# Agent attention and a soft mixture of experts: joining partition maxima by masked products instead of copies, with later combine steps

## The chip, the cores and the metric

The kernel runs on one core of a Trainium2 chip. The metric is the time of one execution on the device in microseconds (us), given as the median of several runs. A profile shows one further execution in detail. Its engines are TensorE (PE; its weight loads are listed as PEld), VectorE (DVE), ScalarE (ACT), GpSimd (POOL) and SyncE (SP), which here only issues transfers. Everything is in 32-bit floating point.

## The reference

B = 4 batches, N = 11456 tokens each, C = 128 channels, 49 agents, 8 experts of 4 slots each (32 slots) and a hidden width of 1024.

```python
def sm(a, b):
    s = scale * (a @ b.transpose(0, 2, 1))
    s = s - s.max(-1, keepdims=True)
    e = np.exp(s)
    return e / (e.sum(-1, keepdims=True) + 1e-09)
agent_v = sm(agents, k) @ v              # agents look at all tokens
x = sm(q, agents) @ agent_v              # tokens look at the agents
...
logits = x @ phi                         # (B*N, 32)
d = softmax of logits over all tokens    # dispatch
slot_input = d.T @ x
for e in range(E):
    h = np.maximum(slot_input[e] @ w1[e], 0.0)
    slot_out[e] = h @ w2[e]
c = softmax of logits over the 32 slots  # combine
return c @ slot_out
```

So there are three softmaxes: over all keys of a batch (49 rows), over the 49 agents for every token, and two over the logits, one down all 45824 tokens and one across the 32 slots. The first and the dispatch one need a maximum that runs over partitions as well as along them.

## The kernel before

**Layout.** The tokens of a batch are cut into four streams. A cell is 32 tokens of each stream, so 128 tokens, and a batch has 90 cells. A group is 16 cells (10 in a batch's last), so a batch has six groups of keys and six of queries, 24 of each in all. With 32 columns of weights, four products write the four quadrants of 32 partitions of one PSUM tile, one for each stream.

**Key side, one group** (function `k_ops`; names as in the order list): `kx` and `kv` load, `ks` makes scores of 64 padded agents in two halves of 32 (line 219), `km` takes the negated maximum of each half along the row (L249). The four quadrants hold the same agents for different tokens, so their maxima must be joined and the result spread to all quadrants again. `kt` moves three quadrants' values to the first with three ScalarE copies (L255), `kr` reduces them together with the running maximum (L261, VectorE), `kn` spreads the result with three more ScalarE copies (L267). Then `ke` takes exponentials (L272), `ka` the rescaling factor, `kT` transposes on VectorE (L283), `kE` multiplies with the values (L290), and `kA` accumulates. After a batch's last group `kg` and `kh` form the agents' values and their product with phi.

**Query side, one group** (`q_ops`): `qx` load, `qs` scores, `qt` transposes, `qm` maxima, then either `qE` (exponentials on ScalarE cell by cell with a sum, L430) or `qu`, `qe`, `qd` (GpSimd, ScalarE, VectorE); `qw`, `qr`, `qN` normalise, `qp` and `qc` transpose through TensorE, `ql` makes the logits (L466), `qM` takes their maximum along the row (L479), `qv` transposes them into a buffer `lt` (L471). The combine softmax follows: `cr` maxima over the slots (L484, VectorE), `cu` subtraction into the result array `x_all` (L487, GpSimd), `ce` exponential in place (L492, ScalarE).

**Rounds** (`r_ops`). One or two query groups form a round, 13 in all. `r2` brings the quadrants' logit maxima together (three ScalarE copies, L536), `r3` reduces (L539), `r4` spreads (three copies, L544), `r5` transposes, `ru`, `re`, `rg` subtract, exponentiate and multiply into the dispatch sums, which `rc` copies out.

**Tail.** The rounds are rescaled to a common maximum, the slot inputs go through the experts (`mh`, `mr`, `mt`, `mc`, `mo`), and `sob` holds the slots' outputs. The output loop then runs over 24 chunks of 16 cells (8 in the first and the last two): `o_sum`, `o_eps`, `o_rec`, `o_mul` normalise the combine weights in `x_all`, `o_tr` transposes them, four products make an output tile of four PSUM banks (L933), VectorE copies one bank (L937), ScalarE three (L938), and a store follows (L942). The first 6 chunks' `o_sum` to `o_mul` (token names `os`, `oe`, `or`, `om`) and 4 transposes (`ot`) stand ahead of the loop.

**The order.** Every engine executes its instructions in the order in which they are issued. That order is written out by hand in a list of tokens, `ORDER` (lines 48 to 101). It holds all steps up to the output loop. Each step names what it depends on, and which buffer it takes and gives back (`BUFS`). The loads are in this list too, and go through SyncE's queue.

Of the kernel before, what the change touches and what calls it, by code (L numbers as in the profile page):

```python
# [7 lines left out]
F32 = mybir.dt.float32  # L8
# [46 lines left out]
ke.1 kx kT.0 qu qe km.1 qE.0 kT.1 km.0 ka@3 qE.3 qe kE kt ka kr kn kA qd ks.1 kE kA qw ke.0 km.1
kt kv ks.0 ka kx ke.1 qd kT.0 qN qE.1 qw@5 kr qw qc.0 qr ks.1 km.0 kT.1 km.1 qp.1@2 kn kE kv cx
kA kt qc.1 qp.0 ke.0 qN qp.1 kA qp.0 ks.0 qc.1@2 qc.0 qr kT.0 ke.1 kT.1 kE qc.1 ka kr kn ke.0 kA
qx km.0 ks.1 km.1 kg.1 kh.1 kt kT.0 kg.2 qp.1 ke.1 kr qx kh.2 kh.5 kg.3 kh.4 kT.1 kh.3 qs.0 qt.0
qr kn qs.1 ql qt.1 ql qm qs.0 qc.0 qv qN kx ke.0 kx qs.1 qE.2 ka ks.0 qu qM qt.0 qE.3 kT.0 ks.1
ke.1 qc.1 qt.1 kv ql qN qp.0 kx qv qc.0 km.0 qM km.1 r2 qp.1 kT.1 qM qc.1 cr ks.0 kt r3 ql qe kr  # L60
ks.1 kn qM qm kv ke.0 ke.1 km.0 cu qp.0 km.1 qv kE r4 kA kx ks.0 qE.0 r5 qp.1 qd kT.0 qc.0 kt qw
kr ql r2 qE.1 ka kn ks.1 r3 ru.0 kT.1 qw kE qr qr km.0 ka kv ke.0 ke.1 qv kv qM qc.1 ks.0 qE.2
qN@7 ks.1 km.1 qN kt kT.0 ru.1 ql r4 kE km.0 kr qE.3 kn qx km.1 re.0 kT.1 kA qM cr@3 kt qv@5 kA
kE r2 kr ke.0 kx qv qw qr kx cr ke.1 r3 qp.0@7 kT.0 r5 qp.1 qN ka kn qc.0@7 qp.0 rg.0 qc.0 ka
qs.0 qs.1 kT.1 ce qc.1 qt.0 qt.1 qp.0 r4 ke.0 ks.0 kT.0 ke.1 ru.0 qm qu re.1 cu@3 ks.1 km.0 ks.0
kv qc.0 km.1 km.0 kT.1 rg.1 re.0 ks.1 kv qx@11 kt kA cr qp.1 ce@3 qe qx kr km.1 cu ru.1 kn qc.1
kx cr ke.0 qd kE qw kE cr qx ke.1 kt kx qr kT.0 qs.0@11 kA kA cu@4 qN qs.1@11 rc kr qp.1@6 kg.1
qt.0@11 qt.1@11 r5 kg.2 cu qm@11 re.1 qc.1@6 qp.0 kn rg.0 ru.0 kh.1 kT.1 qs.0 kv ce qx ke.0 kh.2
kT.0 qt.0 qs.1 kh.5 kh.4 qt.1 kg.3 qu kh.3 qp.1 kv rg.1 qm ql ks.0 qM ke.1 km.0 re.0 ks.1 qs.0
qv qe qc.0 ru.1 km.1 qE.0 ql re.1 qc.1 qs.1 qd ql qt.0 kT.1 kt ql rc qM qt.1 qx kr qE.1 qM qE.2  # L70
qE.3 qw kn qv@8 qm qr qw r2 kx qM qv qr rg.0 ke.0 ks.0 rg.1 rc r3 ka@14 qE.0 kE ke.1 r2 r4 cu kA
ka qE.1 qN kT.0 km.0 cr r5 ks.1 qs.0 qN qs.1 qp.0 r3 ce@4 ru.0 cr r4 kT.1 km.1 qp.0 re.0 qt.0 kx
# [941 lines left out]
```

## Time and profile before

| what | us |
|---|---|
| median of 3 runs (lowest, highest) | 307.31 (306.68, 308.25) |
| the profiled execution's own time | 306.44 |
| its span in the profile | 304.6 |
| TensorE busy, its weight loads | 246.4, 126.4 |
| VectorE busy | 227.1 |
| ScalarE busy | 244.3 |
| GpSimd busy | 126.9 |

The span runs from the first to the last instruction in the trace; the execution's own time has 1.8 us more around it. Busy time is the union of an engine's instructions. A matmul's row is about 0.2 to 0.9 us long, but many overlap, so a group of matmuls takes far less than their number times that mean. In a row of a window, "x" gives the number of instructions, and a bracket at its end gives the engine's idle time before it and what ended it. In a row of groups, the two numbers before the second bar are busy time in us and the mean of one instruction in ns. In a row of waits, "X <- Y: total, times, longest" says for how long X stood idle until Y was done. A total of shares "by line" is of the chain of work that ended last, followed back through what released each step.

### The profile page before, as it was taken

The page shows a single profiled execution, that of the slowest core. Times are in us where ns is not written, and L with a number is a line of the kernel's source. Part 1 is how long each engine was busy: PE and PEld are TensorE (multiplying, and loading weights), DVE is VectorE, ACT ScalarE, POOL GpSimd, SP SyncE. Part 2 cuts the span into 40 slices and gives each one's busy share as a digit, 9 for nine tenths or more (in the row PEclk, how much of TensorE's full clock was granted, in tenths as well). Part 3 has the DMA queues.
Part 4 walks back from the last instruction along what each step waited for, and adds up shares of the span by engine and source line. Part 5 has one row for each costly group of instructions (what it writes and reads, how often), then busy time and mean ns, then how long its engine had stood idle before and what let it go on. Part 6 is the DMA issues. An engine that isn't in the chain of part 4 may idle for free.

```text
span 304.6 us, 8492 instructions
## 1 busy us (share of the span) xinstructions
PE 246.4 (81%) x3236; PEld 126.4 (42%) x3236; DVE 227.1 (75%) x490; ACT 244.3 (80%) x898; POOL 126.9 (42%) x136
## 2 busy tenths in 40 slices
PE   4668888999779998889998998979889965586830
PEld 1113245735463645434554364565665611121200
DVE  0567988499687999768998897788857599678620
ACT  2397899798997999989999999999967587566550
POOL 0010352231445833336742827568859134344200
PEclk9999999999999999979999999999979999556575
DMA  7999999999999997998999988729900079999996
GB/s 237 422 423 417 415 367 384 413 422 340 410 421 385 419 417 267 411 366 303 357 352 341 421 344 310 274 99 388 425 13 2 2 319 420 413 424 417 421 421 267
DMA packets 16023, 104.09 MB, mean 342 GB/s; under 512 B 1904, under 2 KB 2160, under 8 KB 4720
## 3 DMA queue, kind: packets, MB, share of 16 engines
q1 hardware_dynamic: 15840, 103.49, 84.9%
q8 instruction: 25, 0.41, 0.5%
q14 instruction: 14, 0.11, 0.1%
q10 hardware_dynamic: 144, 0.07, 0.1%
HBM read 79.96 MB, written 23.59 MB: 340 GB/s over the span
## 4 chain that ended last, share of the span: by engine, by line
ACT 37%; DMA 21%; PE 17%; DVE 15%; issue 4%; POOL 2%; SPq 2%; DVEq 0%; ACTq 0%
DMA out<-ot 10%; ACT pt L430 9%; DMA qt<-qT 7%; ACT es L272 5%; DMA w2s<-w 4%; PE sq L219 3%; ACT pT L460 3%; PE ev L290 3%; ACT mxs L267 3%; ACT mxs L255 2%; PE sk L219 2%; DVE ot L937 2%; ACT x_all L430 2%; DVE et L283 2%; PE tp L453 2%
## 5 line engine op out<-in xcount | busy, mean ns | idle before, releaser
L219 PE MATMUL sk<-kt,ag 128*32 128x512 f32 (+1 forms) x384 | 49.7, 588 | 12.4 <-DMA kt<-kT 6.1
L219 PE MATMUL sq<-qt,ag 128*32 128x512 f32 (+1 forms) x384 | 46.1, 572 | 7.7 <-DMA qt<-qT 3.9
L933 PE MATMUL po<-ct,sob 32*128 32x512 f32 (+1 forms) x192 | 35.8, 827 | 16.6 <-ACT ot L938 16.4
L938 ACT COPY ot<-po 128x1536 f32<-128x1536 f32 (+1 forms) x24 | 32.6, 1358 | 20.6 <-DVE ot L937 19.2
L430 ACT ACTIVATE pt<-pt,mx 128x49 f32<-128x49 f32 x144 | 46.4, 329 | 0.2
L290 PE MATMUL ev<-vt,et 128*64 128x129 f32 x720 | 44.3, 276 | 1.5 <-PE ev L290 0.9
L290 PEld LDWEIGHTS ev<-vt,et 128*64 128x64 f32 x720 | 39.3, 136 | 9.9 <-issue 3.9
L553 POOL TENSOR_TENSOR dt<-lt,mb 128x512 f32<-128x512 f32 (+1 forms) x24 | 29.2, 1226 | 33.0 <-DVE mb L548 14.1
L445 POOL TENSOR_TENSOR pt<-pt,rt 128x784 f32<-128x784 f32 (+1 forms) x19 | 26.6, 1400 | 28.4 <-DVE rt L441 22.5
L249 DVE TENSOR_REDUCE mxs<-sk 128x1 f32<-128x512 f32 (+1 forms) x48 | 30.4, 642 | 10.0 <-PE sk L219 9.4
L789 POOL TENSOR_TENSOR x_all<-x_all,cd 128x512 f32<-128x512 f32 (+1 forms) x24 | 23.8, 994 | 30.7 <-DVE cd L784 30.7
L283 DVE STREAM_TRANSPOSE et<-es 128x512 f32<-128x512 f32 (+1 forms) x48 | 31.3, 655 | 6.3 <-ACT es L272 6.0
L272 ACT ACTIVATE es<-sk,mxs 128x512 f32<-128x512 f32 (+1 forms) x48 | 30.7, 656 | 0.4
L460 ACT COPY pT<-tp 100x512 f32<-100x512 f32 (+1 forms) x48 | 25.7, 556 | 2.8 <-PE tp L453 2.0
L937 DVE COPY ot<-po 128x512 f32<-128x512 f32 (+1 forms) x24 | 15.6, 648 | 16.5 <-DMA out<-ot 14.3
L430 ACT ACTIVATION_READ_ACCUMULATOR pt<-pt,mx 128x1 f32 x144 | 27.8, 193 | 0.0
L933 PEld LDWEIGHTS po<-ct,sob 32*128 32x128 f32 x192 | 9.6, 234 | 42.5 <-ACT ot L938 42.0
L402 DVE STREAM_TRANSPOSE pt<-sq 128x512 f32<-128x512 f32 (+1 forms) x38 | 25.0, 657 | 2.3 <-PE sq L219 1.6
L487 POOL TENSOR_TENSOR x_all<-lt,rm 128x512 f32<-128x512 f32 (+1 forms) x24 | 23.7, 998 | 6.8 <-DVE m_all L539 4.6
L219 PEld LDWEIGHTS sk<-kt,ag 128*32 128x32 f32 x384 | 10.7, 110 | 31.7 <-ACT es L272 9.7
L453 PE MATMUL tp<-cs,pt 128*100 128x128 f32 x140 | 21.3, 286 | 2.7 <-DVE acc L296 2.3
L466 PE MATMUL lq<-pT,bd_m 100*32 100x256 f32 (+1 forms) x384 | 22.8, 367 | 0.5 <-ACT bd_m L334 0.3
(114 smaller groups left out, 425.2 us busy)
## 6 DMA issues: line engine op xcount, KB each, us to landing
out<-ot SPq DMA_DIRECT2D x21, 1024.0 KB, 7.4
vt<-vL SPq DMA_DIRECT2D x20, 1032.0 KB, 10.0
qt<-qT SPq DMA_DIRECT2D x20, 1024.0 KB, 9.4
kt<-kT SPq DMA_DIRECT2D x19, 1024.0 KB, 8.9
w2s<-w SPq DMA_DIRECT2D x4, 1024.0 KB, 7.6
w1s<-w SPq DMA_DIRECT2D x4, 1024.0 KB, 12.0
vt<-vL SPq DMA_DIRECT2D x4, 645.0 KB, 7.1
qt<-qT SPq DMA_DIRECT2D x4, 640.0 KB, 10.3
```

What stands on the lines that cost most here:

```text
L219: t_.matmul(sp[32 * q4:32 * q4 + 32, :nt], ag[:, b, 32 * h:32 * h + 32], xv[:, q4, :], start=True, stop=True)
L249: v_.tensor_reduce(out=mxs[i % 6][:, 2 * h, 0:1], in_=k["s"][h][:, :nt], axis=AX.X, op=ALU.max, negate=True)
L272: s_.activation(out=k["e"][:, h, :nt], in_=k["s"][h][:, :nt], func=AF.Exp, bias=k["nm"][:, 2 * h:2 * h + 1])
L283: v_.transpose(out=k["et"][:, :n, 32 * h:32 * h + 32], in_=k["e"][:, h, :nt].rearrange("p (t a) -> p t a", a=32))
L290: t_.matmul(k["ev"][o:o + 64, :], k["et"][:, c, :], k["v"][:, c, :], start=c < 2, stop=c >= n - 2)
L430: s_.activation(out=x, in_=x, func=AF.Exp, bias=q["mx"][:, c:c + 1], accum_out=q["rt"][:, c:c + 1])
L445: nc.gpsimd.tensor_tensor(out=x, in0=x, op=ALU.mult, in1=q["rt"][:, :n].unsqueeze(2).to_broadcast([P, n, A]))
L453: t_.transpose(q["tp", h][:, (c - h0) // 2, :], q["pt"][:, c:c + 2, :].rearrange("p c a -> p (c a)"), ident)
L460: s_.copy(out=q["pT"][:, h0 // 2:h1 // 2, :], in_=q["tp", h][:, :(h1 - h0) // 2, :])
L553: nc.gpsimd.tensor_tensor(out=q["dt"][:, :n], in0=q["lt"][:, :n, :], op=ALU.subtract, in1=r["mb"].unsqueeze(1).to_broadcast([P, n, S]))
L933: t_.matmul(po[:, r, :32 * n], z["sob"][32 * r:32 * r + 32, :], z["ct", j][32 * r:32 * r + 32, :32 * n], start=True, stop=True)
L938: s_.copy(out=ov[:, 1:4], in_=po[:, 1:4, :32 * n])
```

## The change

1. The key maxima. `km` writes into a small tile of two columns. A new step `kz` (VectorE) multiplies it with a mask, so that a 128 x 16 operand holds each quadrant's values in its own columns and zeros elsewhere. A new step `kb` (TensorE) multiplies that by a 128 x 32 matrix of stacked identities: four products bring all quadrants' values, and the running maximum, to all four quadrants of a PSUM tile. `kr` reduces that tile in all 128 partitions. The ScalarE copies of `kt` and `kn` go. One ScalarE copy `kp` carries the running maximum into the next group's operand, for all but a batch's last group.
2. The rounds likewise: `r2` is a masked product on VectorE, `r4` four matrix products, `r3` a reduction over all partitions. The copies of `r2` and `r4` go.
3. `qv` writes the logits into `x_all` and the buffers `lt` go; `cr` keeps its maxima in a new array `r_all`, `cu` works in place. The query buffers `pt` grow from 8 to 11. Since the first five query groups keep their weights in the end of `x_all` for a while, the last six `qv` wait for the rounds that read them.
4. `cr`, `cu` and `ce` of the last 8 query groups leave the order list and stand in the output loop, one group in every second chunk. Those of the others now come after `ru` of their group.
5. The output tile of four PSUM banks becomes two tiles of one and three banks. The chunks are 4, 4, 8, then 21 of 16, and 8; 7 chunks instead of 6 are normalised ahead of the loop.
6. The order list is written anew from end to end (not shown below: it has the same steps but for those named).

```diff
@@
+LATE = 8
@@ constants: CO_QD holds a 128x4 mask of the quadrants, loaded with the first part
 BUFS = {
-    "kt": 2, "vt": 3, "qt": 3, "es": 1, "et": 2, "pt": 8, "pT": 3, "lt": 5, "dt": 2,
+    "kt": 2, "vt": 3, "qt": 3, "es": 1, "et": 2, "pt": 11, "pT": 3, "dt": 2,
@@
-CHUNKS = [8] + [16] * 21 + [8, 8]
+CHUNKS = [4, 4, 8] + [16] * 21 + [8]
-NORM = 6
+NORM = 7
@@
+    msk = cs[:, CO_QD:CO_QD + 4]
+    zs = [keep.tile([P, 5, 4], F32, name=f"zs{i}") for i in range(4)]
+    for t in zs:
+        v_.memset(t[:, 4], 0.0)
@@ k_ops
-        def kt():
-            m = mxs[i % 6].rearrange("p (h e) c -> p h e c", e=2)[:, :, 0, :]
-            for r in range(1, 4):
-                s_.copy(out=m[0:32, :, r], in_=m[32 * r:32 * r + 32, :, 0])
+        def kz():
+            sh = [P, 4, 2, 2]
+            v_.tensor_tensor(out=zs[i % 4][:, 0:4].rearrange("p q (h e) -> p q h e", e=2),
+                             in0=k["mx"].unsqueeze(1).unsqueeze(3).to_broadcast(sh),
+                             in1=msk.unsqueeze(2).unsqueeze(3).to_broadcast(sh), op=ALU.mult)
+
+        def kb():
+            c = 5 if g else 4
+            k["mt"] = tile_("a", [P, 3, c], f"mt_{i}")
+            for r in range(4):
+                t_.matmul(k["mt"][32 * r:32 * r + 32], sel_st,
+                          zs[i % 4][:, 0:c, r % 2:r % 2 + 3].rearrange("p q x -> p x q"),
+                          start=True, stop=True)
         def kr():
...
+            k["nm"] = sm.tile([P, 3], F32, name=f"nm_{i}", tag="nm")
+            v_.tensor_reduce(out=k["nm"], in_=k["mt"], axis=AX.X, op=ALU.min)
-        def kn():
-            w = k["nm"] = mxs[(i + 1) % 6][:, :, 4]
-            for r in range(1, 4):
-                s_.copy(out=w[32 * r:32 * r + 32, 0:3], in_=w[0:32, r % 2:r % 2 + 3])
+        def kp():
+            s_.copy(out=zs[(i + 1) % 4][0:32, 4].rearrange("p (h e) -> p h e", e=2),
+                    in_=k["nm"][0:32, 0:3:2].unsqueeze(2).to_broadcast([32, 2, 2]))
@@ q_ops
-            q["lt"] = tile_("lt", [P, QC, S], f"lt_{i}")
-            v_.transpose(out=q["lt"][:, :n, :].rearrange("p c s -> p (c s)"),
+            v_.transpose(out=x_all[:, at:at + n].rearrange("p c s -> p (c s)"),
...
+              [("rg", R0[0] + (j // 2), j % 2) for j in range(AHEAD) if i >= NT - 6],
@@ r_ops
         def r2():
-            x = r["cm"][:, :len(grp)]
-            for q4 in range(1, 4):
-                s_.copy(out=x[0:32, :, q4], in_=x[32 * q4:32 * q4 + 32, :, 0])
+            sh = [P, 4, len(grp)]
+            r["z"] = sm.tile([P, 4, 2], F32, name=f"rz_{ri}", tag="rz")
+            v_.tensor_tensor(out=r["z"][:, :, :len(grp)], op=ALU.mult,
+                             in0=r["cm"][:, :len(grp)].unsqueeze(1).to_broadcast(sh),
+                             in1=msk.unsqueeze(2).to_broadcast(sh))
+        def r4():
+            r["t"] = tile_("a", [P, 4, len(grp)], f"t_{ri}")
+            for q4 in range(4):
+                t_.matmul(r["t"][32 * q4:32 * q4 + 32], sel_st, r["z"][:, :, :len(grp)],
+                          start=True, stop=True)
         def r3():
...
+            v_.tensor_reduce(out=m_all[:, ri:ri + 1], axis=AX.XY, op=ALU.max, in_=r["t"])
-        def r4():
-            for q4 in range(1, 4):
-                s_.copy(out=m_all[32 * q4:32 * q4 + 32, ri:ri + 1], in_=m_all[0:S, ri:ri + 1])
...
+            if qi < NT - LATE:
+                c = op("cr", (qi,), "V", q["c"][0], deps=(("qv", qi),))
+                c = op("cu", (qi,), "G", q["c"][1], deps=(c, f))
+                op("ce", (qi,), "A", q["c"][2], deps=(c,))
@@ output loop
-            po = psO.tile([P, 4, 512], F32, name=f"po_{j}", tag="o")
+            pa = psO.tile([P, 512], F32, name=f"pa_{j}", tag="oa")
+            pb = psO.tile([P, 3, 512], F32, name=f"pb_{j}", tag="ob")
...
-            v_.tensor_copy(out=ov[:, 0], in_=po[:, 0, :32 * n])
-            s_.copy(out=ov[:, 1:4], in_=po[:, 1:4, :32 * n])
+            v_.tensor_copy(out=ov[:, 0], in_=pa[:, :32 * n])
+            s_.copy(out=ov[:, 1:4], in_=pb[:, :, :32 * n])
+            if j % 2 == 0 and j < 2 * LATE:
+                for fn in qs[NT - LATE + j // 2]["c"]:
+                    fn()
```

More of the change, by code (lines that the diff above doesn't have):

```diff
@@ L55 @@
[L55 to L60, printed above, removed]
@@ L171, in tile_agent_attn_soft_moe @@
     x_all = keep.tile([P, B * NCELL, S], F32, name="x_all")
+    r_all = keep.tile([P, B * NCELL], F32, name="r_all")
     g_all = keep.tile([P, NR, A1], F32, name="g_all")
     m_all = keep.tile([P, NR + 1], F32, name="m_all")
-    mxs = [keep.tile([P, 4, 5], F32, name=f"mxs{i}") for i in range(6)]
+    msk = cs[:, CO_QD:CO_QD + 4]
+    zs = [keep.tile([P, 5, 4], F32, name=f"zs{i}") for i in range(4)]
     av = keep.tile([A, B, C], F32, name="av")
@@ L348, in k_ops @@
         before = [("kr", i - 1)] if g else []
-        t = o("kt", (), "A", kt, deps=[m1])
-        r = o("kr", (), "V", kr, deps=[t] + before)
-        bn = o("kn", (), "A", kn, deps=(r,))
+        z_ = o("kz", (), "V", kz, deps=[m1] + ([("kb", i - 4)] if i > 3 else []))
+        t = o("kb", (), "P", kb, deps=[z_] + ([("kp", i - 1)] if g else []), takes=("a",))
+        bn = o("kr", (), "V", kr, deps=[t] + before, gives=(("a", t),))
+        if not last:
+            o("kp", (), "A", kp, deps=[bn] + ([("kb", i - 3)] if i > 2 else []))
         e0 = o("ke", (0,), "A", lambda: ke(0), deps=(bn,), takes=("es",),
@@ L521, in q_ops @@
         f = o("qM", (), "V", qM, deps=[l0] + before, gives=(("a", l0),))
-        v = o("qv", (), "V", qv, deps=(f,) if last else (l0,), takes=("lt",),
+        v = o("qv", (), "V", qv, deps=[f if last else l0] +
+              [("rg", R0[0] + (j // 2), j % 2) for j in range(AHEAD) if i >= NT - 6],
               gives=(("a", l0),))
-        f = o("cr", (), "V", cr, deps=(v,))
-        f = o("cu", (), "G", cu, deps=(f,), gives=(("lt", v),))
-        o("ce", (), "A", ce, deps=(f,))
+        q["c"] = [lambda: cr(), lambda: cu(), lambda: ce()]
     def r_ops(ri):
@@ L573, in o @@
             return op(fam, (ri,) + sub, eng, fn, **kw)
-        f = o("r2", (), "A", r2, deps=[("qM", q["i"]) for q in grp])
-        f = o("r3", (), "V", r3, deps=(f,))
-        f = o("r4", (), "A", r4, deps=(f,))
+        f = o("r2", (), "V", r2, deps=[("qM", q["i"]) for q in grp])
+        f = f4 = o("r4", (), "P", r4, deps=(f,), takes=("a",))
+        f = o("r3", (), "V", r3, deps=(f,), gives=(("a", f4),))
         mb = o("r5", (), "V", r5, deps=(f,))
@@ L880, in tile_agent_attn_soft_moe @@
     end = o("zz", "P", lambda: None,
-            deps=[k for k in ops if k[0] == "ce"] + [("rg", NR - 1, 0), hq["r", 1, 1]])
+            deps=[("rg", NR - 1, 0), hq["r", 1, 1]])
     s_ops(1, 1)
@@ L904, in tile_agent_attn_soft_moe @@
     cut1 = 1 + max(n for n, k in enumerate(order) if k in ends)
-    cut2 = 1 + max(n for n, k in enumerate(order) if k == end or k[0] in ("ce", "rg"))
     def emit(part):
```

145 lines of the change are left out of this document (74 added, 71 removed).

## The prediction

> **What bounds the kernel now.** I read first the busy time of each engine by stage: columns are the stretch, its length, then busy time (and instructions) of TensorE, its weight loads, VectorE, ScalarE and GpSimd, the granted clock, the DMA share and GB/s.
>
> ```profile
> 0.00:50.00 50.00, 36.70 (x352) 14.49 (x356) 31.70 (x59) 34.27 (x158) 8.88 (x13) 1.00 0.95 378
> 50.00:205.00 155.00, 140.34 (x2085) 78.91 (x2082) 129.34 (x279) 145.13 (x599) 73.90 (x78) 0.99 0.90 356
> 205.00:242.00 37.00, 33.61 (x613) 23.44 (x611) 27.16 (x74) 30.09 (x101) 26.10 (x28) 0.95 0.43 173
> 242.00:304.60 62.60, 35.78 (x192) 9.61 (x192) 38.94 (x80) 34.77 (x43) 17.99 (x18) 0.70 0.91 377
> ...
> 150.00:180.00 30.00, 27.72 (x422) 14.09 (x413) 26.66 (x55) 29.42 (x124) 15.18 (x17) 1.00 0.93 363
> ...
> 205.00:220.00 15.00, 13.55 (x262) 8.94 (x260) 12.84 (x34) 14.39 (x57) 12.69 (x15) 1.00 0.97 394
> ```
>
> There are four stages with four limits. The first 50 us wait for loads (DMA 0.95). From 50 to 205 us ScalarE is the fullest engine, 145.1 of 155 us (94%), and 98% from 150 to 180; but TensorE stands close behind with 140.3 (91%), the DMA engines at 0.90 and VectorE at 129.3 (83%). From 205 to 242 us come the last batch's logits, weights and experts, a chain with ScalarE at 14.4 of 15 us at its start. From 242 us on the store queue is the limit (0.91).
>
> Next the chain that ended last, cut to 50 to 205 us, and who waits there:
>
> ```profile
> by line: ACT pt L430 16.9%; ACT es L272 9.0%; PE ev L290 6.2%; ACT pT L460 6.1%; ACT mxs L267 5.1%; PE sk L219 4.8%; PE sq L219 4.3%; ACT mxs L255 4.0%; DVE et L283 3.8%; PE tp L453 3.8%; ACT dt L558 3.7%; ACT cm L536 3.4%; issue 3.0%; ACT
> ...
> PE sk L219 <- ACT es L272: 4.8, 5, 1.7
> PE sq L219 <- ACT es L272: 1.8, 3, 0.9
> ...
> DVE mxs L261 <- ACT mxs L255: 4.9, 8, 1.1
> DVE m_all L539 <- ACT cm L536: 4.1, 4, 1.4
> ...
> ACT mxs L255 <- DVE mxs L249: 1.0, 2, 0.8
> ```
>
> The small ScalarE copies of the maxima (L255, L267, L536) hold 12.5% of this stage's chain, 19.4 us. TensorE waits 6.6 us for exponentials that stand behind them on ScalarE.
>
> **The change, part by part.**
>
> *The copies that go.* Busy time of L255, L267, L536 and L544 from 50 to 205 us, then of L536 and L544 from 205 to 242 us (columns: ScalarE busy, clock, DMA share, GB/s):
>
> ```profile
> 50.00:205.00 155.00, 10.66 (x56) 0.99 0.90 356
> 50.00:205.00 155.00, 11.12 (x57) 0.99 0.90 356
> 50.00:205.00 155.00, 5.21 (x27) 0.99 0.90 356
> 50.00:205.00 155.00, 5.11 (x27) 0.99 0.90 356
> 205.00:242.00 37.00, 2.29 (x12) 0.95 0.43 173
> 205.00:242.00 37.00, 2.27 (x12) 0.95 0.43 173
> ```
>
> That is 32.1 us off ScalarE in the main stage and 4.6 us in the next. What comes back is kp, one copy of the same kind for each group but a batch's last, about 16 in the stage at L267's 0.195 us: 3 us. ScalarE falls to about 116 of 155 us and stops being the limit there. So the gain is not 32 us: it ends where the next engine is full.
>
> *The products that come, on TensorE.* Each kb and each r4 is four products of 32 columns of weights. In the trace each product of this precision is two instructions, so eight. The nearest row has the same shape with 50 columns instead of 15 (gp); a short group that stands by itself (gte) is the dear end:
>
> ```profile
> 216.28 0.56 PE L566 MATMUL gp<-pt,dt 128*32 128x50 f32 x32 [0.52 <-ACT g_all L570]
> 219.69 1.02 PE L657 MATMUL gte<-cs,g_all 128*50 128x32 f32 x18 [0.36 <-DVE m_all L539]
> ```
>
> 0.56 / 32 = 0.0175 us each, 0.14 us for eight; 1.02 / 18 = 0.057 us, 0.45 us for eight. The stage has about 18 kb and 9 r4 (27 copies of L536, three a round): 3.8 to 12.2 us. I take 3.8, the same shape; TensorE then has 144.1 us of work in the stage. The Trainium skill (TensorEngine Tiling (Array Packing), Key Properties) says that a change of tiling mode drains TensorE, and kb stands among products of 64 and 128 columns. If each drained, the dear end would hold and the stage would keep only 2.5 us of slack. No row here separates that drain.
>
> *The steps on VectorE.* kz and r2 replace nothing on this engine: about 27 small products of two SBUF operands. kr and r3 change rows, not count; kr costs what its old form shows:
>
> ```profile
> L261 DVE TENSOR_REDUCE mxs<-mxs 32x4 f32<-32x20 f32 x20 | 3.1, 154 | 6.0 <-ACT mxs L255 5.9
> ...
> 227.09 1.05 POOL L789 TENSOR_TENSOR x_all<-x_all,cd 128x512 f32<-128x512 f32 x1
> 227.52 0.80 DVE L661 TENSOR_TENSOR g_all<-g_all,wrs 128x150 f32<-128x150 f32 x1 [0.59 <-ACT g_all L570]
> ...
> 232.25 1.05 POOL L789 TENSOR_TENSOR x_all<-x_all,cd 128x512 f32<-128x512 f32 x1
> 232.38 0.15 DVE L716 TENSOR_REDUCE gs<-g_all 128x1 f32<-128x4 f32 x1
> 232.56 0.75 DVE L717 SCALAR_TENSOR_TENSOR gs<-gs,wrs 128x1 f32<-128x1 f32 x1
> ```
>
> The cheap end is 0.15 us. The dear end is L717: one element takes 0.75 us, from 232.56 to 233.31, and it ends when the GpSimd instruction beside it ends (233.30). L716, with one tensor operand, runs in 0.15 us under the same GpSimd instruction. So a VectorE step with two SBUF operands seems to wait out GpSimd. The Trainium skill (SBUF — State Buffer, SBUF: two separate sides) states this as a lock: VectorE with two SBUF inputs and GpSimd exclude each other for a whole instruction. These rows agree. GpSimd is busy 73.9 of 155 us (48%), so an average kz or r2 costs 0.15 + 0.48 x 0.6 = 0.44 us, 12 us in the stage: VectorE 141 us. That nearly equals TensorE's 144.
>
> *What that gives the main stage.* Three resources (TensorE 144, VectorE 141, DMA 0.90 x 155 = 140) become the limit together. ScalarE as the limit filled 94% of the stage, at best 98%; at the middle, 96%, TensorE's 144.1 us take 150 us: a gain of 5. Ends: nothing (TensorE at 153, or 94%), and 14 (the chain's 19.4 us less 27 x 0.2 us for the product that takes the copies' place on it).
>
> *The new wait.* kb stands in TensorE's fixed order behind kz. What is queued behind it are other groups' scores, transposes and kE, and for those VectorE and ScalarE wait in turn. Before, the copies stood in the same place on ScalarE and waited for the same maximum only 1.0 us in the stage. I cost the wait at under 1 us, with ends zero and the last rival's.
>
> *The first 50 us.* Here the chain of the window reads:
>
> ```profile
> by line: DMA qt<-qT 44.4%; ACT x_all L430 13.0%; PE sq L219 7.7%; SPq L212 6.3%; ACT es L272 4.8%; issue 3.8%; ACT x_all L417 3.2%; ACT mxs L255 3.1%; ACT pt L430 2.5%; ACT mxs L267 2.0%; DVE x_all L402 1.5%; DVE acc L296 1.2%; DVE mxs L249
> ```
>
> Both copies stand there too, but loads end most waits. I take a gain of 1 (ends 0 and 2.5: L255 and L267 hold 5.1% of that window's chain). The constants' first load grows by 36 columns, four memsets come: both lie before the first score.
>
> *205 to 242 us.* The 4.6 us of copies leave a ScalarE that is 96% full at first, and each of the four last rounds loses two triplets of copies that stood in series, for which VectorE waited:
>
> ```profile
> DVE mb L548 <- ACT m_all L544: 1.3, 3, 0.6
> ...
> DVE m_all L539 <- ACT cm L536: 0.9, 2, 0.6
> ...
> L492 ACT ACTIVATE x_all<-x_all 128x512 f32<-128x512 f32 (+1 forms) x17 | 9.2, 595 | 0.1
> L487 POOL TENSOR_TENSOR x_all<-lt,rm 128x512 f32<-128x512 f32 (+1 forms) x9 | 8.7, 985 | 2.2 <-DVE rm L484 2.2
> ...
> L484 DVE TENSOR_REDUCE rm<-lt 128x16 f32<-128x512 f32 (+1 forms) x9 | 5.4, 614 | 0.0
> ...
> L566 PE MATMUL gp<-x_all,dt x160: 205/208/233, 92.0 to 116.0; 128*32 128x50 f32 x160
> ```
>
> Nine of cr and cu and 17 of ce ran in this stage; eight groups' leave for the output loop, so up to 5 us of VectorE and ScalarE and 8 us of GpSimd go too. But the logits, the last rounds and the experts remain a chain. I take 3 (ends 0 and 5). qv now writes into the result array and needs no buffer of its own. The last six wait for the rounds that read the first groups' weights out of that array (gp from x_all, over at 116 us here): nearly 90 us earlier, so that wait costs nothing.
>
> *The output loop.*
>
> ```profile
> 243.46 0.80 ACT L938 COPY ot<-po 128x768 f32<-128x768 f32 x1 [1.36 <-DVE ot L937]
> ...
> 244.29 29.98 SPq L942 DMA_DIRECT2D out<-ot  x14
> ...
> 249.41 0.65 DVE L937 COPY ot<-po 128x512 f32<-128x512 f32 x1
> 251.30 0.65 DVE L937 COPY ot<-po 128x512 f32<-128x512 f32 x1
> ...
> 271.70 0.69 DVE L937 COPY ot<-po 128x512 f32<-128x512 f32 x1 [0.40 <-DMA out<-ot]
> 274.12 0.69 DVE L937 COPY ot<-po 128x512 f32<-128x512 f32 x1 [0.41 <-DMA out<-ot]
> ```
>
> Free of stores VectorE makes a chunk in 1.89 us; stores allow one each 2.42 us. A late cr in every second chunk adds 0.61 / 2 = 0.3 us: 2.2, still under 2.42, so stores hide it, with 0.2 us to spare. If that cover is gone (late cr, cu and ce on the path), eight times 0.6 us: 5 us. ScalarE's 1.44 us copy with half a 0.6 us ce fits too. The PSUM split lets the first product go before ScalarE's copy, which is worth nothing while stores lead. A first chunk of 4 cells halves its copies and starts the stores some 0.7 us sooner. Taken: 0.5 gain (ends 1.5 gain, 3 loss).
>
> Sum: 1 + 5 + 3 + 0.5 = 9.5 us. The profiled execution took 306.4 us (span 304.6), giving 296.9; the median of the runs is 0.9 above it, so I expect 297 to 298 and say 297.
>
> **The rivals.**
> - *VectorE becomes the limit through GpSimd.* If GpSimd is nearly always in the way, 27 x 0.75 us = 20 us come to VectorE: 149.6 us, full at 96% in 156. The main stage gains nothing, the other parts 4.5: 302 us. For it: L717. Against: VectorE ends a wait as soon as GpSimd does, and GpSimd is busy less than half the time. By the skill's lock it would go this way only with denser GpSimd work.
> - *The chain shortens in full.* 14 us in the main stage and the dear ends elsewhere (2.5 + 5 + 1.5): 23 us, 284; half way to it 289. For it: 19.4 us of this stage's chain. Against: three resources above 83%.
> - *Nothing moves*: the DMA engines already lead from 50 to 205 us. Against: their 0.90 follows buffers that compute frees. Time 307.
> - *Slower: TensorE waits at kb.* TensorE has 155 - 144 = 11 us of slack for 27 waits, so above 0.4 us each the stage grows. At 0.75 us (what L717 took, if kz meets that each time) it is 20 us, 9 more than the slack; less 4.5 elsewhere, 311. For it: TensorE would stop for all its other work. Against: the 1.0 us that ScalarE waited in that place.
>
> **How the numbers follow.** Forecast (291 to 300) 0.50; VectorE limit 0.18; chain in full 0.15; nothing 0.07; slower 0.10. About half a per cent, 1.5 us, is what can be told from no change. The first three are faster: 0.83, same 0.07, slower 0.10. The range 286 to 307 leaves out the far end of the chain's rival and the slower one.
>
> **What would show it.** ScalarE near 75% between 50 and 205 us while TensorE passes 93%; the loads' end earlier by 5 to 6 us; kb of 0.2 to 0.4 us and kz spread from 0.15 to above 0.7 us; no new TensorE wait for kz above 0.4 us on average; the output stage 62 us as before with its period at 2.4 us. I am wrong if TensorE shows many waits for kz or kp, if the output period passes 2.5 us, or if ScalarE stays above 90%.

## The result and the profile after

The changed kernel takes 295.9 us (median; 292.74 to 304.15), beside 307.78 us (306.68 to 309.36) for the kernel before on the same chip: a ratio of 0.958, 95% interval 0.948 to 0.967. (Runs over 1.5% above the fastest of their kernel are left out of the ratios here, so a ratio isn't the quotient of the medians.) The prediction was 297.0 (286 to 307). The profiled execution took 295.61 us, span 293.6. Here and in the runs below the granted matmul clock after the first 200 us varies from one execution to the next. So main stages are compared by a moment that lies mostly before that: the start of the product `agv`, with which the key side's sums leave. From the start of the span to `agv` the granted clock averages 0.98 to 1.00 in all of them. Each run has one profile, so a difference of 2 or 3 us in this moment is not much: seven profiles with the same main stage differ by 2.6 us.

That product in the kernel before, and in the changed kernel (start, duration, engine, line):

```profile
205.03 0.38 PE L308 MATMUL agv<-acc,cs 128*100 128x129 f32 x2
```

```profile
192.05 0.46 PE L323 MATMUL agv<-acc,cs 128*100 128x129 f32 x2
```

The changed kernel by stage (columns as in the prediction: TensorE, weight loads, VectorE, ScalarE, GpSimd, clock, DMA share, GB/s):

```profile
0.00:50.00 50.00, 36.23 (x360) 14.35 (x362) 31.58 (x68) 25.90 (x119) 8.77 (x13) 0.97 0.95 380
50.00:192.05 142.05, 140.07 (x2279) 83.71 (x2274) 133.80 (x304) 114.06 (x459) 69.26 (x73) 1.00 0.93 380
...
150.00:180.00 30.00, 30.00 (x450) 17.61 (x452) 29.21 (x65) 25.91 (x109) 13.78 (x15) 1.00 0.87 354
...
192.00:231.00 39.00, 36.17 (x726) 26.60 (x725) 27.70 (x76) 22.49 (x71) 22.93 (x25) 0.91 0.47 191
231.00:293.60 62.60, 44.99 (x184) 17.07 (x183) 43.32 (x89) 37.47 (x50) 25.92 (x26) 0.73 0.92 377
```

From 50 us to `agv` TensorE is busy for 140.07 of 142.05 us (98.6%), and without a gap from 150 to 180 us. VectorE stands at 94%, ScalarE has fallen from 94% to 80%. The chain that ended last in that stretch, of the changed kernel, has no ScalarE line among its longest; it is TensorE's own work:

```profile
by line: PE ev L305 20.6%; PE sk L227 15.6%; PE sq L227 14.9%; PE tp L470 9.8%; PE lq L483 7.0%; DVE pt L419 3.3%; DVE kmx L259 3.2%; DVE et L298 2.5%; issue 2.5%; DVE x_all L487 2.4%; DVE mx L424 2.2%; PE gp L584 2.0%; DVE cm L495 2.0%; PE
```

By stage, in the two profiled executions (the slots' outputs `sob` are made at 241.74 before and 229.49 after):

| stage | before | after | gain | predicted |
|---|---|---|---|---|
| start to `agv` | 205.0 | 192.05 | 13.0 | 1 + 5 |
| `agv` to `sob` | 36.7 | 37.4 | -0.7 | 3 |
| `sob` to the end | 62.9 | 64.1 | -1.2 | 0.5 |
| span | 304.6 | 293.6 | 11.0 | 9.5 |

The stages are not quite alike: of the `gp` instructions on TensorE 488 stand ahead of `agv` before and 424 after, so 64 of them, 0.8 us, moved from the first row to the second.

So the sum came out and its terms did not. Three things are to be explained: why the main stage gained twice as much, why the experts' stage gained nothing, and what the output loop lost.

### The profile page after: what moved, and what is told of

It is laid out like the page before. It is cut to its first block, busy times and chain, and to the rows that moved or that the text cites. A ratio compares the mean times of both kernels' runs of the same rounds, so it can differ in the third digit from the quotient of the medians.

```text
span 293.6 us, 8944 instructions
## 1 busy us (share of the span) xinstructions
PE 257.4 (88%) x3540; PEld 141.7 (48%) x3540; DVE 236.4 (81%) x535; ACT 199.9 (68%) x698; POOL 126.9 (43%) x137
## 4 chain that ended last, share of the span: by engine, by line
PE 50%; DVE 21%; DMA 17%; ACT 3%; issue 3%; POOL 1%; SPq 1%; DVEq 0%; ACTq 0%; POOLq 0%
PE ev L305 11%; PE sq L227 10%; PE sk L227 9%; DMA out<-ot 9%; PE tp L470 5%; DMA qt<-qT 5%; PE lq L483 4%; DMA kt<-kT 3%; ACT ot L958 2%; PE gp L584 2%; DVE pt L419 2%; DVE cd L799 2%; DVE kmx L259 2%; DVE ot L957 2%; DVE x_all L487 2%
## 5 line engine op out<-in xcount | busy, mean ns | idle before, releaser
L287 ACT ACTIVATE es<-sk,nm 128x512 f32<-128x512 f32 (+1 forms) x48 | 30.3, 653 | 27.0 <-DVE nm L278 21.6
L958 ACT COPY ot<-pb 128x1536 f32<-128x1536 f32 (+2 forms) x25 | 32.5, 1303 | 10.4 <-DMA out<-ot 10.2
L259 DVE TENSOR_REDUCE kmx<-sk 128x1 f32<-128x512 f32 (+1 forms) x48 | 30.3, 642 | 10.9 <-PE sk L227 10.4
L571 POOL TENSOR_TENSOR dt<-x_all,mb 128x512 f32<-128x512 f32 (+1 forms) x24 | 29.2, 1224 | 22.5 <-DVE mb L566 8.4
L953 PE MATMUL pa<-ct,sob 32*128 32x512 f32 (+2 forms) x50 | 34.3, 782 | 3.7 <-DVE ot L957 3.3
L953 PE MATMUL pb<-ct,sob 32*128 32x512 f32 (+2 forms) x150 | 34.0, 772 | 2.3 <-ACT ot L958 2.2
L810 POOL TENSOR_TENSOR x_all<-x_all,cd 128x512 f32<-128x512 f32 (+2 forms) x25 | 23.9, 961 | 15.9 <-DVE cd L805 15.9
L503 POOL TENSOR_TENSOR x_all<-x_all,r_all 128x512 f32<-128x512 f32 (+1 forms) x24 | 23.8, 1000 | 12.4 <-DVE r_all L499 12.4
L429 POOL TENSOR_TENSOR pt<-pt,mx 128x784 f32<-128x784 f32 (+1 forms) x10 | 13.1, 1305 | 28.8 <-DVE mx L424 28.8
L957 DVE COPY ot<-pa 128x512 f32<-128x512 f32 (+2 forms) x25 | 15.5, 620 | 11.9 <-DMA out<-ot 10.3
```

The lines of the kernel that those rows point to most:

```text
L259: v_.tensor_reduce(out=k["mx"][:, h:h + 1], in_=k["s"][h][:, :nt], axis=AX.X, op=ALU.max, negate=True)
L287: s_.activation(out=k["e"][:, h, :nt], in_=k["s"][h][:, :nt], func=AF.Exp, bias=k["nm"][:, 2 * h:2 * h + 1])
L571: nc.gpsimd.tensor_tensor(out=q["dt"][:, :n], in0=x_all[:, q["at"]:q["at"] + n], op=ALU.subtract, in1=r["mb"].unsqueeze(1).to_broadcast([P ...
L953: t_.matmul(pb[:, r - 1, :32 * n] if r else pa[:, :32 * n], z["sob"][32 * r:32 * r + 32, :], z["ct", j][32 * r:32 * r + 32, :32 * n], star ...
L958: s_.copy(out=ov[:, 1:4], in_=pb[:, :, :32 * n])
```

## The main stage: the products, or the order?

The change puts products in place of copies and writes the order list anew. Theories: the copies on ScalarE were the cost, or the order was. The first three runs swap one at a time. Each reads as its edit, the expectation, and what came.

**Old key copies in the new order.**

```diff
-        kz (VectorE), kb (TensorE), kr, kp
+        kt (three ScalarE copies, at kz's place), kr, kn (three copies, behind kr)
```

> The changed kernel, with only the key maxima joined and spread by ScalarE copies again (kt and kn in the places of kz and kr; kb and kp gone); the new order, buffers, rounds' products, late steps and chunks stay. Copies theory (the gain comes from taking the small copies off ScalarE and off the chain): ScalarE gets 24 x 6 x 0.193 - 20 x 0.176 = 24 us back, some 18 of them between 50 and 196 us, 136 of 146 us there, and the chain of every group waits on it again, so the main stage grows by 5 to 9 us: 301 to 305 us. Order theory (the gain is the new order's and the larger buffers'): ScalarE has 28 us of idle time in that stage for 18 us of copies, TensorE stays full, and the time stays at 295 to 297 us.

316.09 us (313.84 to 316.87), ratio 1.036 (1.025 to 1.046): slower than the kernel before, outside what either theory gave. `agv` starts at 205.43, where the kernel before has 205.03. So up to there the gain is gone; what makes it slower than the kernel before comes later (42.1 us from `agv` to `sob`, with the clock at 0.80, against 36.7 at 0.95). Waits of this kernel from 50 to 205 us (total, times, longest):

```profile
PEld sq L223 <- ACT es L276: 10.9, 9, 2.8
...
ACT mxs L259 <- DVE mxs L253: 8.1, 7, 2.2
...
ACT mxs L271 <- DVE mxs L265: 7.6, 11, 1.1
...
PE sq L223 <- ACT es L276: 7.0, 8, 1.8
```

ScalarE now waits 15.7 us for maxima at its two groups of copies (1.0 us at the first of them in the kernel before), and TensorE behind it for exponentials. Placed like this, copies do not pay in the new order. The placing itself may be part of it: `kn` follows `kr` directly in all 24 groups here, in the kernel before by 1 to 17 places (median 3.5). A new order with room for the copies was not run.

**Old round copies in the new order.**

```diff
-        r2 (VectorE product), r4 (TensorE), r3 (all partitions)
+        r2 (three ScalarE copies), r3, r4 (three ScalarE copies)
```

> The changed kernel, with only the rounds' maxima joined and spread by ScalarE copies again (78 copies x 0.19 us = 15 us on ScalarE, 10 us of them before 196 us, the rest in the last rounds). Copies theory: the rounds feed GpSimd and later steps with slack before 196 us, so little is lost there, 0 to 1 us, and the last four rounds lose 0.5 us each: 296 to 299 us. Order theory: no change, 295 to 297 us.

301.65 us (295.41 to 303.58), ratio 0.977 (0.968 to 0.985), where the changed kernel had 0.958 (0.948 to 0.967) and, in another batch of runs below, 0.968 (0.960 to 0.976). `agv` starts at 195.08, where seven profiles with the changed kernel's main stage have 191.33 to 193.97. The rounds' half is worth 1 to 4 us by that moment; the interval overlaps the second of these, so the time does not separate it. The key half is the large one.

**The key products in the old order.**

```diff
-        kt, kr, kn at their places in the old list
+        kz at kt's place, kb directly ahead of kr, kp at kn's place
```

> The kernel before, with only the key maxima's masked products (kz in kt's place, kb just ahead of kr, kp in kn's place; at two groups kr moves by one or two places for want of a free PSUM tile). Everything else, the order included, is the old. Copies theory: ScalarE falls from 145 to about 127 of 155 us in the main stage and the time by 4 to 7 us: 300 to 304 us. Order theory: the old order has TensorE reach kb before kz is done and gives the time back: 306 to 310 us.

302.24 us (300.52 to 305.36), ratio 0.987 (0.972 to 1.001). The time lies in the copies theory's range; but the interval holds 1, so a gain is not shown, and `agv` starts at 205.41, no earlier than with copies. Its waits and its stage:

```profile
DVE nm L274 <- PE mt L268: 10.0, 12, 3.2
ACT zs L277 <- DVE nm L274: 8.5, 6, 3.6
...
PE mt L268 <- DVE zs L260: 5.9, 5, 2.9
```

```profile
50.00:205.41 155.41, 144.93 (x2241) 85.73 (x2237) 133.08 (x297) 123.27 (x499) 73.44 (x78) 0.97 0.90 357
```

The copies are gone and ScalarE is at 79%, yet VectorE waits 10.0 us at `kr` for the product, ScalarE 8.5 us at `kp` for what `kr` makes, and TensorE 5.9 us at `kb` for the mask step, as the order theory has it. The clock has a share: it averages 0.97 in this stage and 0.99 in the kernel before, which is worth up to 3 us (0.02 x 155). So with these placings neither the products nor the order alone shortens the stage by more than about 3 us (205.4 both times); together they take 13.0 us off (11.1 to 13.7 over seven profiles with this main stage). In the changed kernel the same three waits, from 50 to 192 us, are:

```profile
ACT es L287 <- DVE nm L278: 6.3, 7, 2.5
...
DVE nm L278 <- PE mt L272: 2.2, 2, 2.0
...
PE mt L272 <- DVE zs L264: 1.7, 3, 0.7
...
ACT zs L281 <- DVE nm L278: 1.2, 1, 1.2
```

What differs in the two lists is the room, counted in places (1 is directly behind). From `kz` to `kb` the median is 5 in both. From `kb` to `kr` it is 1 in every group of the last experiment, and 1 to 14, median 6, in the changed kernel. That gave the next run.

**The changed kernel with kb directly ahead of kr.**

```diff
-        kz ... kb ... kr        (kb to kr: 1 to 14 places)
+        kz ......... kb kr      (kb to kr: 1 place, all 24 groups; nothing else moved)
```

> The changed kernel with one edit in the order list: every kb stands directly ahead of its kr, where the changed kernel has 1 to 14 other steps (median 6) between them. Distance theory: what the new order gives the products is this distance. VectorE's wait for the product, 2.2 us in the main stage of the changed kernel and 10.0 us in the kernel before with the key products (which has the two side by side in every group), comes back to 8 us or more, and the last kg product starts at 198 to 203 us instead of 192 to 194; the time is 300 to 305 us. Rival (the rest of the order matters, the distance does not): the wait stays below 4 us, the last kg product starts by 195 us, and the time is 294 to 298 us.

306.45 us (302.56 to 308.32), ratio 0.999 (0.991 to 1.006). `agv` starts at 200.47; two waits in the main stage and the stage itself:

```profile
ACT es L285 <- DVE nm L276: 11.4, 9, 4.4
...
DVE nm L276 <- PE mt L270: 9.3, 10, 1.7
```

```profile
50.00:200.47 150.47, 143.22 (x2294) 85.16 (x2290) 135.21 (x306) 115.31 (x467) 69.28 (x73) 1.00 0.89 360
```

The distance theory holds: `agv` and the wait fall where it put them (the time 1.5 us above its range). TensorE idles 7.3 us of the stage instead of 2.0, and is busy longer for the same work (179.3 us for the 2634 matmul instructions ahead of `agv`, against 176.3). The distance from product to reduction makes 6.5 to 9.1 us up to `agv`, of the 11.1 to 13.7 gained there. Of the time's gain nothing measurable is left: the interval holds 1 and lies clear of the changed kernel's. The wait goes on, too: ScalarE's exponentials wait 11.4 us for `nm`, the result of `kr`, where the changed kernel had 6.3. Two things stay open. `agv` is still 4.6 us earlier than in the kernel before, so the distance is not all of the stage's gain. And the other way round, the old order with room between `kb` and `kr`, was not run; there the waits at `kp` and `kb` would have to go as well, which this run does not bring back.

## The mask steps and GpSimd

The prediction took VectorE steps with two SBUF operands to wait out GpSimd. If the second operand is what matters, a multiplication by a per-partition number should be free of it.

**One tensor operand.**

```diff
-  v_.tensor_tensor(out=zs, in0=mx (spread), in1=msk (spread), op=mult)
+  for h in range(2): v_.tensor_scalar(out=zs half h, in0=msk, scalar1=mx[:, h], op0=mult)
   (r2 likewise, one for each group of the round)
```

> The changed kernel, with kz and r2 each made of one or two VectorE steps whose only tensor operand is the mask, the maximum being a scalar for each partition (48 steps for kz, 24 for r2). Lock theory (a VectorE step with two operands in SBUF waits out the GpSimd instruction beside it): the longest kz, 0.95 us, and the longest r2, 1.22 us, fall to under 0.25 us, the steps cost about 0.13 us each, and the time changes by less than 1.5 us (295 to 297), since what VectorE saves in waits it pays in the extra steps. Rival (these spreads have another cause, such as the queue ahead of them): durations up to 0.9 us remain.

`agv` starts at 203.85, 11.8 us later than in the changed kernel; the lowest run is 306.1 and the median 313.01 (to 315.02), too scattered for a ratio. The mask steps of the changed kernel and then of this one (ns, min/median/max):

```profile
L264 DVE TENSOR_TENSOR zs<-kmx,cs x24: 110/170/952, 11.4 to 183.1; 128x16 f32<-128x16 f32 x24
```

```profile
L264 DVE TENSOR_SCALAR zs<-cs,kmx x48: 128/223/1608, 9.7 to 192.7; 128x8 f32<-128x8 f32 x48
```

In this kernel, one short step on VectorE, and GpSimd beside it:

```profile
218.32 1.23 DVE L551 TENSOR_SCALAR rz<-cs,cm 128x4 f32<-128x4 f32 x1
```

```profile
216.65 2.87 POOL L570 TENSOR_TENSOR dt<-x_all,mb 128x512 f32<-128x512 f32 x2 [1.42 <-PE gp L583]
```

Four elements take 1.23 us and end at 219.55, GpSimd at 219.52. The mask steps over 0.35 us, 20 here and 10 in the changed kernel, all end within 0.05 us of the end of a GpSimd instruction. So the step with one tensor operand waits out GpSimd too, and there are nearly twice as many of them: `zs` and `rz` keep VectorE busy for 23.4 us of the main stage, 9.4 in the changed kernel. With 14 us more on VectorE the stage is 11.8 us longer, so at 94% VectorE has little slack; the steps that wait for the maxima lie behind it (exponentials wait 14.5 us for `nm`, 6.3 in the changed kernel). The Trainium skill (SBUF — State Buffer, SBUF: two separate sides) lists two kinds of VectorE step under its lock, those with two SBUF inputs and those in a mode that uses both ports. My prediction drew only on the first; the rows of this run agree with a lock that takes in more than the first, and cannot tell the mode.

**The mask steps on ScalarE.**

```diff
-  v_.tensor_scalar(out=zs half h, in0=msk, scalar1=mx[:, h], op0=mult)
+  s_.activation(out=zs half h, in_=msk, func=Copy, scale=mx[:, h])
```

> The changed kernel, with the masked products kz and r2 on ScalarE (two copies scaled by a column for a kz, one or two for an r2, 0.29 us each: 72 copies, 21 us) instead of VectorE. VectorE theory (VectorE, 94% full in the main stage, sets the time beside TensorE, and its 12.8 us of masked products with their waits for GpSimd cost time): VectorE loses 12.8 us, no masked product lasts over 0.35 us, and the time falls by 1 to 5 us. ScalarE theory (any step of the maxima on ScalarE stands behind its long exponentials and holds TensorE's kb up): TensorE waits for zs by more than 5 us in the main stage instead of 1.7, and the time rises by 4 to 12 us.

`agv` starts at 195.86, 1.9 us after the latest of the changed kernel's main stages; 303.91 us (295.49 to 305.94), with only one run below 300 and so no ratio. Neither theory came out as written: the stage is not shorter, though VectorE falls to 128.8 of 145.9 us, and TensorE does not wait over 5 us for the masks. The steps of `kz` take an even 0.284 to 0.324 us here, with no lock, but ScalarE waits for the maximum at them:

```profile
ACT zs L264 <- DVE kmx L259: 7.7, 11, 1.9
...
DVE nm L278 <- PE mt L272: 5.7, 6, 2.0
```

The place that is free of GpSimd is the place that the copies had just left.

## The output loop

**The changed kernel again**, beside the next three.

> The changed kernel itself, so that the next three are compared with it on one chip. Both theories: 0.95 to 0.97 of the kernel before, 62.6 us from the first store to the end, with the stores short of work in the first 6 us.

297.07 us (294.05 to 301.23), ratio 0.968 (0.960 to 0.976); 63.5 us from the first store to the end, a little over the expectation.

After the first store, the first 8 us of the changed kernel (2 us each; last column GB/s), and the first 4 us of the kernel before:

```profile
231.00:233.00 2.00, 1.69 (x10) 0.64 (x9) 2.00 (x6) 0.46 (x1) 1.07 (x2) 1.00 0.35 127
233.00:235.00 2.00, 1.41 (x15) 0.92 (x16) 2.00 (x4) 1.93 (x6) 0.70 (x1) 1.00 0.31 113
235.00:237.00 2.00, 1.52 (x15) 0.59 (x8) 2.00 (x5) 2.00 (x3) 1.05 (x1) 1.00 0.72 285
237.00:239.00 2.00, 1.82 (x11) 0.31 (x6) 2.00 (x6) 1.34 (x4) 1.76 (x2) 1.00 1.02 418
```

```profile
244.30:246.30 2.00, 1.43 (x12) 0.60 (x16) 2.00 (x5) 1.55 (x2) 0.00 (x0) 1.00 0.60 244
246.30:248.30 2.00, 1.35 (x12) 0.34 (x12) 2.00 (x5) 1.65 (x3) 1.05 (x1) 1.00 0.84 346
```

The changed kernel stores too little for 6 us, since the first late group is taken up at the first chunk. In its timeline the late `ce` (L508) goes ahead of ScalarE's output copy, after a wait for the late `cu`:

```profile
231.46 1.05 POOL L503 TENSOR_TENSOR x_all<-x_all,r_all 128x512 f32<-128x512 f32 x1 [7.10 <-DVE r_all L499]
...
232.54 0.63 ACT L508 ACTIVATE x_all<-x_all 128x512 f32<-128x512 f32 x1 [1.55 <-POOL x_all L503]
...
233.08 1.16 ACT L958 COPY ot<-pb 128x384 f32<-128x384 f32 x2
```

**Late groups from chunk 4 on.**

```diff
-            if j % 2 == 0 and j < 2 * LATE:
+            if j % 2 == 0 and 4 <= j < 4 + 2 * LATE:
...
(the group's index moves with it: j - 4 in place of j)
```

> The changed kernel, with the late combine steps in chunks 4, 6, ... 18 of the output loop instead of 0, 2, ... 14. Late theory (the output stage lost 2.3 us because the first chunks' ScalarE copies stand behind a ce that waits for GpSimd): the stores get over 300 GB/s in their first 6 us instead of some 175, the stage takes 60 to 61 us and the time falls by 1.5 to 2.5 us. Chunk theory (the small first chunks give the stores too little): the stage stays at 62 to 63 us, the time within 0.7 us.

From the first store to the end it takes 60.7 us, instead of 62.6 and 63.5; the store rate in the first 6 us (mean 328 GB/s, 175 in the changed kernel):

```profile
236.90:238.90 2.00, 2.00 (x21) 1.41 (x23) 2.00 (x4) 1.56 (x4) 0.00 (x0) 1.00 0.56 204
238.90:240.90 2.00, 2.00 (x15) 0.60 (x8) 2.00 (x6) 1.76 (x3) 0.48 (x1) 1.00 0.90 353
240.90:242.90 2.00, 1.62 (x11) 0.57 (x8) 2.00 (x6) 0.85 (x1) 1.25 (x2) 1.00 1.04 426
```

So the late groups' start was the loss in the output loop, about 2 us. All profiles bear it out: 62.2 to 63.6 us in the ten with late groups from chunk 0, 60.7 and 60.8 in the two with late groups from chunk 4, 60.3 and 60.5 in the two without late groups. The time, 297.72 us (295.89 to 304.09), ratio 0.973 (0.965 to 0.981), does not show it. In its profile `agv` to `sob` took 41.4 us, 39.9 in the changed kernel's beside it (the next section).

**The old chunks (8 first, two of 8 last).**

```diff
-CHUNKS = [4, 4, 8] + [16] * 21 + [8]      7 normalised ahead
+CHUNKS = [8] + [16] * 21 + [8, 8]         6 normalised ahead
```

> The changed kernel, with the chunks of before (8, 21 of 16, 8, 8) and six of them normalised ahead of the loop. Chunk theory: the output stage is back at 60.3 us and the time 1.5 to 2 us lower, though the first store comes 0.7 us later. Late theory: the first ScalarE copies still stand behind a waiting ce, the stage takes 62 to 63 us from a first store 0.7 us later: 0 to 1 us slower than the changed kernel.

62.2 us from the first store, as the late theory has it: the small first chunks are not the loss. The time, 299.82 us (293.97 to 303.09), has one run below 299 and so no ratio.

**One output tile of four PSUM banks.**

```diff
-  pa (1 bank), pb (3 banks)
+  po (4 banks)
```

> The changed kernel, with one output tile of four PSUM banks in place of the two of one and three. Theory (stores lead, so the split is worth nothing): within 0.7 us of the changed kernel. Rival (the split lets VectorE and ScalarE copies run side by side while the stores wait for the first chunks): 1 to 2 us slower, with the first 6 us of the stores poorer still.

63.1 us from the first store, with the same 175 GB/s in the first 6 us; 299.58 us (295.11 to 303.32), ratio 0.968 (0.960 to 0.977), the same as the changed kernel's beside it. The split is worth nothing that can be measured, as predicted.

## Between agv and sob: the clock

One stretch of the same program, the last rounds to the slot inputs, in four profiles: the changed kernel, the changed kernel again, late groups from chunk 4, and one output tile. The third number is the stretch's length, the one ahead of the DMA share the granted clock.

```profile
207.00:218.50 11.50, 11.07 (x181) 8.87 (x182) 5.80 (x21) 4.37 (x13) 6.15 (x7) 0.70 0.35 139
```

```profile
208.00:220.80 12.80, 12.80 (x189) 10.09 (x186) 5.92 (x21) 4.38 (x13) 6.15 (x7) 0.57 0.32 130
```

```profile
209.00:222.60 13.60, 13.60 (x181) 10.72 (x180) 5.70 (x21) 4.38 (x13) 6.15 (x7) 0.50 0.29 116
```

```profile
209.00:217.90 8.90, 7.97 (x178) 6.36 (x177) 5.85 (x22) 4.27 (x13) 6.17 (x7) 1.00 0.41 165
```

VectorE, ScalarE and GpSimd do the same work in all four (5.7 to 5.9, 4.3 to 4.4, 6.2 us); the stretch takes 8.9 us at full clock and 13.6 us at half. Ahead of it stands the longest gap of TensorE there, in the changed kernel and with the same 1.78 us in the three others:

```profile
206.73 0.25 PE L558 MATMUL t<-rz,cs 128*32 128x4 f32 x8 [1.78 <-DVE rz L551]
```

This `rz` is a mask step that waits out GpSimd (1.22 us for four elements). The gap is the same where the clock then falls and where it doesn't.

What differs is where the gap lies. In all 14 profiles the granted clock is 1.00 or 0.50 and changes only at moments that lie whole multiples of 3.41 us apart. The step of that length with the gap, and the step behind it, in the changed kernel; then the two steps that share the gap, and the one behind them, with one output tile:

```profile
204.59:208.00 3.41, 1.63 (x59) 1.43 (x48) 3.38 (x6) 0.96 (x5) 1.99 (x2) 1.00 1.01 408
208.00:211.41 3.41, 3.41 (x54) 2.57 (x57) 2.79 (x13) 2.26 (x7) 1.27 (x1) 0.50 0.81 332
```

```profile
204.02:207.43 3.41, 2.67 (x106) 1.96 (x106) 2.96 (x8) 2.49 (x8) 3.03 (x3) 1.00 1.02 418
207.43:210.84 3.41, 2.36 (x70) 1.96 (x70) 2.96 (x10) 1.02 (x5) 0.97 (x1) 1.00 1.00 411
210.84:214.25 3.41, 3.00 (x80) 2.52 (x78) 2.75 (x11) 2.59 (x10) 3.12 (x5) 1.00 0.50 204
```

Where one step holds all or most of the gap, TensorE is busy for 1.63 to 1.88 us of it (changed kernel, its repeat, late groups from chunk 4), and the clock halves with the next step. Where two steps share it, the clock stays here; with the old chunks (2.66 and 2.32 us busy) it falls. Between `agv` and `sob` each step with TensorE busy for less than 1.95 us, six in all profiles, is followed by half clock, while steps with 1.95 to 2.45 us are followed by either. So the same gap costs the clock or not by its place on this grid, and no sharp limit is shown. The Trainium skill (TensorE: Matmul & The Clock Gate, What's actually happening) has the gate judge activity in windows of about 3.4 us that run freely. The steps of 3.41 us, which lie differently in each execution, agree with that.

**Filler products in the gap.** The kernel already has filler products (`fl`, results unused); four more go ahead of the last `r4`.

```diff
-FILL = (0, 3, 3, 2, 2, 2, 1)        ... en rg.1 r2@12 r4@12
+FILL = (0, 7, 3, 2, 2, 2, 1)        ... en rg.1 r2@12 fl fl fl fl r4@12
```

> The changed kernel, with four more filler steps on TensorE (eight transposes of the identity whose results nobody reads, some 0.9 us) just ahead of the r4 of the last round, where TensorE stood idle 1.8 us behind an r2 that GpSimd held up. Clock theory (the tail's length follows the granted clock, which fell to 0.5 to 0.7 in most executions after that idle stretch): the clock between the last keys and the experts' input stays near 1.0, the stretch takes 9 us instead of 11.5 to 13.6, and the time falls by 2 to 4 us against the changed kernel, with less spread. Rival (the clock falls for what comes later, or by chance): the clock stays at 0.5 to 0.7 in that stretch and the time is unchanged or 0.5 us worse.

The gap shrinks to 0.76 us. In the profiled execution the clock stays full through this stretch (40 slices of the span, tenths) and `agv` to `sob` takes 35.7 us instead of 37.4:

```profile
PEclk9999999999999999999999999999999779867575
```

But the runs scatter as before, 296.39 us (293.29 to 302.2), ratio 0.966 (0.954 to 0.977), so no gain in time is shown.

**Late groups from chunk 4, and fillers.** Both edits together.

> The changed kernel with both: late combine steps in chunks 4, 6, ... 18, and the four filler steps. If the two causes are what was read from the traces, the output stage takes 60 to 61 us and the tail 35 us, and the time is 3 to 5 us below the changed kernel (291 to 293 us, 0.950 to 0.960 of the kernel before). If the clock theory falls, only the output stage's 2 us remain: 294 to 296.

294.74 us (292.59 to 297.9), ratio 0.967 (0.954 to 0.979). The output loop takes 60.8 us again, but the clock falls in this profile too. It stays at 1.00 behind the filled gap (the step that holds it has TensorE busy for 2.63 us) and halves two steps later, behind one with 2.03 us, which has a gap of 1.25 us at `gp`. So the fillers mend one gap and the next one takes its place. The time lies where the expectation has it if the clock theory falls. It is the lowest median of all, and its interval covers the changed kernel's: no better version is shown.

## Why the prediction was right, and where it was wrong

- **The bound.** ScalarE and its copies led the main stage; with them gone TensorE leads, at 98.6% (forecast: above 93%). ScalarE's work is 114.1 us, forecast 116.
- **The products' price** was sized low: `kb` 4.87 and `r4` 1.99 us of TensorE in the stage, 6.9 instead of 3.8, still far below the dear end of 12.2. The old order with key products has 144.9 us where the kernel before has 140.3; its clock was lower (0.97, 0.99), so that difference is not the products' price alone.
- **The mask steps** cost VectorE 9.4 us, forecast 12. The wait for GpSimd is real; that it needs two SBUF operands fell.
- **The step that failed** is "at the middle, 96%, TensorE's 144.1 us take 150 us". The stage is 98.6% full, and TensorE is busy only 140.07 us: 144.1 / 0.986 would be 146.1, so 4 of the 8 us that were missed are the share and 4 the work. I took the order as given and costed the operations alone. The room between a step and what needs it decides the share: with `kb` next to `kr` the same operations fill 95% (143.2 of 150.5). Of the work's 4 us, 0.8 are the `gp` that moved behind `agv`, and up to 1.6 the clock, 0.99 in the stage before and 1.00 after. The rest may be room too: TensorE is busy some 3 us longer where `kb` stands next to `kr`.
- **The new wait.** At `kb` TensorE waits 1.7 us (forecast: under 1). I priced that wait and left out the next, VectorE's at `kr` for the product. It is the one that takes the gain away where the order leaves it no room (9.3 and 10.0 us, against 2.2). The slower rival had the right kind of mechanism on the wrong engine; it didn't come about because of the spacing. No row of the kernel before could have told that, but the new list could: `kb` to `kr` can be counted in it.
- **The experts' stage**: 3 us forecast, 0.7 lost. This term failed, and the clock is not the reason. Four profiles have the full clock from `agv` to `sob`. Two of them are the old order with key products, which still has the rounds' copies there, and the changed kernel with one output tile:

```profile
205.41:240.14 34.73, 32.15 (x613) 22.34 (x611) 27.60 (x74) 29.58 (x103) 26.66 (x28) 1.00 0.46 184
```

```profile
193.80:228.86 35.06, 32.11 (x708) 23.53 (x707) 27.35 (x74) 21.04 (x68) 22.97 (x25) 1.00 0.53 212
```

ScalarE's work falls by 8.5 us and the stage does not get shorter. TensorE is the fullest engine, busy for 32.1 us in both, 92 to 93%. The forecast read the stage from ScalarE, 96% full in the first 15 us, and from its copies in series; its own row has TensorE at 33.61 of 37 us. (The second has the 64 `gp` more, 0.8 us.)
- **The output loop**: the period was right, copies at 263.11 and 265.53 are 2.42 us apart, and stores start 1.0 us sooner after `sob` (forecast 0.7). The cover was not right: "stores hide it" holds only once stores lead, and the first late groups come before that.
- **The sum** (11.0 in the spans, 9.5 forecast) is right because a doubled gain met two gains that turned into losses. That the forecast lay so near is partly luck.

## What to carry to other kernels

An operation moved to another engine is worth what the order around it lets it be: with an order written out by hand, count the places between the step, its producer and its consumer on each engine, before and after, and price the wait on both sides. Where work was deferred into a loop that stores hide, it had to start only once the stores led. And before a gain of 1% is sought, see how much one stretch of the same work varies by the clock, and compare stages at the same granted clock.

## What the runs showed of the hardware

- Small VectorE multiplications from SBUF wait out GpSimd whether they have two tensor operands (128x16: 0.11 to 0.95 us) or one and a number for each partition (128x8: 0.13 to 1.61 us); the same on ScalarE takes 0.28 to 0.32 us. The reduction with one tensor operand in the prediction's rows (L716, 0.15 us under GpSimd) did not wait.
- The same TensorE work takes 8.0 us busy at a granted clock of 1.00 and 13.6 at 0.50, after the same gap of 1.78 us. The clock goes by steps of 3.41 us, and between `agv` and `sob` each step in which TensorE is busy for less than 1.95 us is followed by half clock; so one gap is followed by either, by where it lies among the steps.
- With tighter waits around it, TensorE is busy longer for the same 2634 matmul instructions: 179.3 against 176.3 us. Why is not shown.
